# Key-value products of one batch: one wait for two units, or a wait for each

## The chip, the cores and the metric

The kernel runs on one core of a Trainium2 chip. The metric is device time in microseconds (us).

Names in the profile: PE is TensorE, PEld its weight loads, ACT is ScalarE, DVE VectorE, POOL GpSimd, SP SyncE, which issues loads and stores. A name like L540 is line 540 of the kernel. At L540 are the key-value products that this document is about; L705 and L751 are the products with the first and the second weight (line numbers shift by a few from run to run: in the changed kernel these are L541, L703 and L749). `VR` and `VB` are V before and after its cast to bf16, `PS` is a PSUM buffer, `MBLK` the normalized key-value products, `XT` the attention's result, `ESB` the exponentials of the ELU, `qsT` the softmax of Q, transposed. An eviction is a copy out of PSUM.

## The reference, cut to what matters

Linear attention over 8 batches of 8 heads, then two matrix products with an ELU between them:

```python
q_s = softmax(q, axis=-1); k_s = softmax(k, axis=2)         # 576 positions, 64 wide
kv  = np.einsum('bhsd,bhse->bhde', k_s, v)                  # the key-value products
x   = np.einsum('bhsd,bhde->bhse', q_s, kv)                 # then laid out as 4608 x 512
h   = x @ w_in                                              # 512 x 2048
g   = np.where(h > 0, h, np.exp(np.minimum(h, 0)) - 1)
out = g @ w_out                                             # 2048 x 512
```

The last two products are nearly all of the work. The attention of a later batch is worked in between them.

## The kernel before: the parts that matter

A batch is handled as two units of four heads. `kv` records the products of both units as **one** operation of 72 small matmuls (a "stay"), which waits for all that either unit needs:

```python
def kv(self, units, ps, key):
    ...
    def mm(e):
        for x, n in enumerate(units):
            ek, VB = self.ek(n % 2), self.VB[n % 2]
            for c in range(CH):                      # 9 chunks
                for f in range(2):
                    for h in range(2):
                        ...
                        last = e.matmul(P[hs, o:o + D + 1], ek[fs, h, c, :],
                                        VB[fs, h, c, 0:D + 1], start=(c == 0), stop=(c == CH - 1))
        return last
    R = []
    for n in units:
        i = n % 2
        R += [f"kR{i}", f"VB{i}0", f"VB{i}1", f"VBone{i}"]
    S.add("pe", len(units) * 270 + 200, mm, key, R=R, X=self.banks(ps), tag=f"kv{units}")
    # ... DVE takes the reciprocals and forms MBLK from the result
```

`kR` is a unit's exponentials of K (made on ACT), `VB` its V in bf16 (cast on DVE or POOL). A scheduler in Python orders all recorded operations. Its `emit` turns dependencies into semaphores: an operation increments its engine's semaphore only if another one needs to know of it, and the increment rides on the operation's last instruction. I call that increment a mark:

```python
            for d in want:
                if kn.get(d.sem.name, 0) >= d.val:
                    continue                              # already known
                self.E[o.eng].wait_ge(d.sem, d.val)
                ...
            ins = o.emit(self.E[o.eng])
            ...
            elif o in needed:
                count[o.eng] += 1
                o.sem, o.val = sems[o.eng], count[o.eng]
                ins.then_inc(o.sem, 1)
```

After a stay the loads of the next batch's K and V go into the same buffers, so each of them waits for the operation that read the buffer last:

```python
for n in units:
    if more:
        loads(n + 2, "kv", key)       # W=[kR.., vR..]: overwrites what the products read
        self.k_part(n + 2, k1)
```

The softmax here doesn't subtract the row's maximum and nothing guards it: scores larger than these inputs give would overflow.

## Time and profile before

| | before |
|---|---|
| device time, median of 3 | 297.22 us (297.14 to 298.07) |
| span of the profiled execution | 295.2 us |
| PE busy | 289.4 us |
| stays of L540, each of 72 matmuls | 7 |
| wait of PE in them | 0.3 us, in the first stay only |

PE is at work for all but 5.8 us of the span, of which 3.0 us come after its last matmul (it ends at 292.17) and 2.5 us in the first 7.6 us. The question is how much of one short wait can be taken away. A matmul is drawn longer than its share of the time, so sums here are made from starts.

### The profile page before, as it was taken

The numbers are of one execution on the slowest core, as the hardware profiler recorded it, in microseconds if no ns is written. First come the engines' busy times: TensorE is split into PE (matmuls) and PEld (weight loads), VectorE is DVE, ScalarE is ACT, GpSimd is POOL, SyncE is SP. The second block draws the span as 40 slices with busy tenths as digits, with TensorE's granted clock in tenths as the row PEclk, the third lists the DMA queues.
The fourth block names the chain that finished last, engine by engine and source line by source line (L and its number), as shares of the span: only waits on it lengthen the run. The fifth ranks groups of instructions, "written<-read, shape, count | busy, mean of one in ns | idle before, by whom it ended". The sixth has DMA issues, their size and how long they took to land.

```text
span 295.2 us, 4381 instructions
## 1 busy us (share of the span) xinstructions
PE 289.4 (98%) x1836; PEld 235.7 (80%) x1836; DVE 151.1 (51%) x173; ACT 152.9 (52%) x179; POOL 123.0 (42%) x135
## 2 busy tenths in 40 slices
PE   6999999999999999999999999999999999999995
PEld 2688878888888788878888888788878888888885
DVE  6757835898356904782368416760661056105600
ACT  5676447935776175636554655536531454125411
POOL 8996201763177025713472237314740055005500
PEclk9999999999999999999999999999999999999999
DMA  7999979979992696049902990098002110230022
GB/s 254 314 393 389 386 251 308 295 235 160 356 196 76 228 340 136 0 132 350 223 0 58 365 276 6 5 344 197 0 0 67 44 34 2 48 75 21 0 67 76
DMA packets 37747, 49.50 MB, mean 168 GB/s; under 512 B 17312, under 2 KB 18624, under 8 KB 37728
## 3 DMA queue, kind: packets, MB, share of 16 engines
q1 hardware_dynamic: 30992, 34.68, 42.3%
q0 software_dynamic: 6272, 14.03, 15.6%
q10 hardware_dynamic: 464, 0.53, 0.5%
q8 instruction: 14, 0.23, 0.3%
q14 instruction: 5, 0.04, 0.0%
HBM read 36.70 MB, written 9.44 MB: 156 GB/s over the span
## 4 chain that ended last, share of the span: by engine, by line
PE 85%; DMA 7%; POOL 6%; issue 0%; DVE 0%; ACT 0%; POOLq 0%
PE PS L751 41%; PE PS L705 39%; DMA VR<-in_v_dram 7%; POOL W L367 3%; PE PS L540 2%; PE PS L635 2%; PE PS L669 1%; POOL W L378 1%; POOL VR L323 1%; POOL KR L323 0%; POOL QR L355 0%; POOL QR L824 0%; POOL KR L344 0%; DVE VB L489 0%; ACT OSB L784 0%
## 5 line engine op out<-in xcount | busy, mean ns | idle before, releaser
L734 DVE SCALAR_TENSOR_TENSOR GT<-ESB,PS 128x1024 fp32r<-128x1024 f32 x68 | 82.7, 1220 | 111.4 <-POOL ESB L731 111.3
L751 PE MATMUL PS<-W,GT 128*128 128x512 f32 (+1 forms) x592 | 136.5, 386 | 0.0
L705 PE MATMUL PS<-XT,W 128*128 128x512 f32 x576 | 132.8, 390 | 0.0
L705 PEld LDWEIGHTS PS<-XT,W 128*128 128x128 f32 x576 | 107.9, 188 | 22.7 <-issue 0.3
L751 PEld LDWEIGHTS PS<-W,GT 128*128 128x128 f32 x592 | 108.0, 188 | 21.6
L731 POOL TENSOR_SCALAR ESB<-ESB 128x1024 f32<-128x1024 f32 x68 | 71.0, 1047 | 100.4 <-ACT ESB L719 100.3
L719 ACT ACTIVATE ESB<-PS 128x1024 f32<-128x1024 f32 x72 | 73.7, 1028 | 49.2 <-PE PS L705 49.2
L765 ACT ACTIVATE OSB<-PS 128x512 f32<-128x512 f32 x35 | 20.6, 599 | 50.5 <-PE PS L751 50.0
L485 POOL CAST VB<-VR 128x1152 bf16<-128x1152 f32 x12 | 14.6, 1216 | 45.7 <-DMA VR<-in_v_dram 45.7
L418 DVE TENSOR_REDUCE ZQ<-QR 128x18 f32<-128x1152 f32 (+1 forms) x16 | 19.1, 1198 | 3.0 <-ACT QR L412 3.0
L432 DVE TENSOR_TENSOR QS<-QR,RZQ 128x1152 f16<-128x1152 f32 x14 | 18.9, 1360 | 0.3
L479 ACT ACTIVATE KR<-KR 128x1152 bf16<-128x1152 f32 x14 | 15.9, 1169 | 4.3 <-DMA KR<-in_k_dram 4.3
L472 POOL CAST qsT<-QR 128x1152 fp32r<-128x1152 f16 x12 | 13.8, 1148 | 9.0 <-DMA QR<-QS 9.0
L412 ACT ACTIVATE QR<-QR 128x1152 f32<-128x1152 f32 (+1 forms) x16 | 16.2, 1038 | 1.0 <-DMA QR<-in_q_dram 0.9
L655 ACT ACTIVATE XT<-PS 128x640 fp32r<-128x640 f32 (+1 forms) x12 | 8.2, 738 | 15.4 <-PE PS L635 15.4
L367 POOL DMA_DIRECT2D W<-in_moe_w_in_dram x16 | 10.0, 1406 | 0.0
L679 ACT ACTIVATE XT<-PS 128x1024 fp32r<-128x1024 f32 (+3 forms) x8 | 6.8, 847 | 5.7 <-PE PS L669 5.7
L691 PE MATMUL PS<-IDLE 128*128 128x512 f32 (+1 forms) x14 | 7.8, 665 | 1.5 <-DVE IDLE L803 1.5
L378 POOL DMA_DIRECT2D W<-in_moe_w_out_dram x6 | 9.0, 2398 | 0.0
L635 PE MATMUL PS<-qsT,MBLK 128*128 128x320 f32 (+3 forms) x32 | 7.1, 337 | 0.0
L691 PEld LDWEIGHTS PS<-IDLE 128*128 128x128 f32 (+1 forms) x14 | 2.6, 209 | 5.5 <-issue 2.4
L540 PEld LDWEIGHTS PS<-VB,KR 64*64 64x64 bf16 x504 | 4.7, 107 | 2.6 <-DVE GT L734 1.8
(52 smaller groups left out, 95.7 us busy)
## 6 DMA issues: line engine op xcount, KB each, us to landing
out_dram<-OSB SPq DMA_DIRECT2D x67, 128.0 KB, 2.4
QR<-in_q_dram SPq DMA_DIRECT2D x12, 576.0 KB, 7.6
KR<-in_k_dram SPq DMA_DIRECT2D x12, 576.0 KB, 6.2
VR<-in_v_dram SPq DMA_DIRECT2D x12, 576.0 KB, 6.9
W<-in_moe_w_in_dram POOLq DMA_DIRECT2D x16, 256.0 KB, 9.2
W<-in_moe_w_out_dram POOLq DMA_DIRECT2D x3, 1024.0 KB, 15.0
KR<-in_k_dram POOLq DMA_DIRECT2D x3, 576.0 KB, 18.2
VR<-in_v_dram POOLq DMA_DIRECT2D x4, 288.0 KB, 13.4
```

The lines of the kernel that those rows point to most:

```text
L367: "gp", 530, lambda e, kc=kc: e.dma_start(self.W1[:, kc, sl], w[kc, :, :, sl]), key,
L412: lambda e, part=part: e.activation(part, part, AF.Exp), key,
L418: S.add("dve", 1350 if n > 1 else 750, lambda e, z=z, src=src: e.tensor_reduce(z, src, AX.X, ALU.add), key, R=self.q_res(n) if n > 1 else ...
L432: S.add("dve", 1400, lambda e: e.tensor_tensor(qso, raw[:, :, :, :], rz, ALU.mult), key, R=qR + [f"RZQ{i}"], W=[f"QS{al}"], low=True, tag= ...
L479: S.add("act", t_act(1152, False), lambda e: e.activation(ek[:, :, :, :], flat.rearrange("p (h c d) -> p h c d", h=2, c=CH), AF.Exp), key, ...
L485: self.cv[n] = S.add("gp", 1250, lambda e: e.tensor_copy(VB[:, :, :, 0:D], raw[:, :, :, :]), key, R=rv, W=[f"VB{i}0", f"VB{i}1"], low=True ...
L705: last = e.matmul(P[:, t * 512:(t + 1) * 512], self.W1[:, kc, tt * 128:(tt + 1) * 128], self.XT[:, kc, rc:rc + BLK], start=(kc == 0), stop ...
L719: S.add("act", t_act(1024, True), lambda e: e.activation(esb[:, :], P[:, :], AF.Exp), key, W=[f"E{i}"], X=self.banks(ps), tag=f"exp{j}.{g}")
L731: S.add("gp", 1120, lambda e: e.tensor_scalar(esb[:, :], esb[:, :], 1.0, 0.0, ALU.min, ALU.max), key, X=[f"E{i}"], tag=f"min{j}.{g}", port ...
L734: S.add("dve", t_dve(1024), lambda e: e.scalar_tensor_tensor(gt, esb[:, :], -1.0, P[:, :], ALU.add, ALU.max), key, R=[f"E{i}"], W=gw, X=se ...
L751: last = e.matmul(dst, GT[:, jj, ts * 128:(ts + 1) * 128], self.W2[:, jj, cols], start=(jj == 0), stop=(jj == 15))
L765: S.add("act", t_act(512, True), lambda e: e.activation(osb[:, :], src, AF.Copy), key, W=[f"O{i}0", f"O{i}1"], X=[f"b{bk}"], tag=f"evo{jb} ...
```

## The change

Intent: the first unit's 36 products should not stand behind the second unit's V, which arrives later. Each unit's products become an operation of their own. The order of matmuls stays as it was.

```diff
-        def mm(e):
-            for x, n in enumerate(units):
-                ek, VB = self.ek(n % 2), self.VB[n % 2]
+        for x, n in enumerate(units):
+            i = n % 2
+
+            def mm(e, x=x, ek=self.ek(i), VB=self.VB[i]):
                 for c in range(CH):
 ...
-            return last
-        R = []
-        for n in units:
-            i = n % 2
-            R += [f"kR{i}", f"VB{i}0", f"VB{i}1", f"VBone{i}"]
-        S.add("pe", len(units) * 270 + 200, mm, key, R=R, X=self.banks(ps), tag=f"kv{units}")
+                return last
+            S.add("pe", 270 if x else 470, mm, key, R=[f"kR{i}", f"VB{i}0", f"VB{i}1", f"VBone{i}"],
+                  X=self.banks(ps), tag=f"kv{n}")
```

## The prediction

> **What bounds the kernel now.** I began with the page's busy times and its slices, then the chain that ended last in order of time, then the waits of PE alone, then the timeline around the one wait that the change can touch. From the page:
>
> ```profile
> PE 289.4 (98%) x1836; PEld 235.7 (80%) x1836; DVE 151.1 (51%) x173; ACT 152.9 (52%) x179; POOL 123.0 (42%) x135
> ...
> PEclk9999999999999999999999999999999999999999
> ...
> PE 85%; DMA 7%; POOL 6%; issue 0%; DVE 0%; ACT 0%; POOLq 0%
> ```
>
> PE is busy for 289.4 of 295.2 us at an undiminished clock; every other engine stands at about half. The chain is PE for 85%; its 7% of DMA lies wholly before 41 us. This is that joint of the chain (start, length, what):
>
> ```profile
> 20.92 19.92 DMA VR<-in_v_dram
> 40.84 0.02 issue
> 40.86 0.48 DVE VB L489
> 41.34 0.04 issue
> 41.38 0.78 PE PS L540 x68
> 42.16 2.05 PE PS L751 x8
> ```
>
> From 41.38 on the chain never leaves PE until the last eviction at 292.21. Behind the joint PE has nothing to wait for, so whatever PE gains here should come off the end undiminished, and nothing gained elsewhere would. The waits of PE, whole run (total, times, longest):
>
> ```profile
> PE PS L691 <- DVE IDLE L803: 1.5, 1, 1.5
> PE PS L513 <- DVE QS L432: 1.0, 1, 1.0
> PE PS L540 <- DVE VB L489: 0.3, 1, 0.3
> ```
>
> Three waits in 295 us, and only the last belongs to the key-value products (L540). There are seven stays of these products, 72 matmuls each, and six of them show no wait of PE. So one stay of seven can gain, the first one. Its timeline, 36 to 43 us:
>
> ```profile
> 36.35 1.17 ACT L479 ACTIVATE KR<-KR 128x1152 bf16<-128x1152 f32 x1 [3.26 <-DMA KR<-in_k_dram]
> 37.43 0.90 ACT L521 ACTIVATE qsT<-PS 128x896 fp32r<-128x896 f16 x1
> 37.86 0.76 DVE L494 CAST VB<-VR 128x1152 bf16<-128x1152 f32 x1 [0.77 <-DMA VR<-in_v_dram]
> ...
> 39.00 2.08 PE L751 MATMUL PS<-W,GT 128*128 128x512 f32 x8
> 39.37 1.16 ACT L479 ACTIVATE KR<-KR 128x1152 bf16<-128x1152 f32 x1 [1.04 <-DMA KR<-in_k_dram]
> ...
> 40.86 0.47 DVE L489 CAST VB<-VR 128x576 bf16<-128x576 f32 x1 [0.28 <-DMA VR<-in_v_dram]
> ...
> 41.38 0.78 PE L540 MATMUL PS<-VB,KR 64*64 64x65 bf16 x72 [0.30 <-DVE VB L489]
> ...
> 42.09 2.12 PE L751 MATMUL PS<-W,GT 128*128 128x512 f32 x8
> ```
>
> The first unit has its exponentials at 37.52 (36.35 + 1.17) and its V at 38.62 (37.86 + 0.76). The second has its exponentials at 40.53 and the last half of its V at 41.33 (40.86 + 0.47). All 72 matmuls wait for that 41.33.
>
> **What the Trainium skill says.** "TensorE: Matmul & The Clock Gate", section "Step-by-step: what each phase is for": matmuls stay in program order, only weight loads are pulled ahead. The trace agrees: the first unit's 36 products, whose V was ready at 38.62, stood until 41.38 behind a wait placed on the first of the 72. "Perfetto Trace Analysis", section "Tensor Engine Instruction (MATMUL, LD_WEIGHTS)": the end of a matmul in a profile is estimated from its size. It shows here: a 128x512 matmul is drawn 0.389 us long, but 64 of them take 14.51 us in the chain, 0.227 each. So I count from start to start, not by the drawn idle of 0.30. Same page, section "Identifying Dependency Chains": a second awaited engine can cost an inserted EventSemaphore instruction. The trace has such records on PE's sequencer of 0.051 us each (one at 40.57, before this stay), beside running matmuls.
>
> **The change part by part.**
>
> Removed: the first unit's products no longer wait for the second unit's V. When would they start? In the stay at 96.5 us, which has no wait of PE, the matmuls before it end in drawing at 96.60 and L540 starts at 96.53, 0.07 us before. In the first stay the matmuls before end at 41.08 (39.00 + 2.08), so an unhindered start is 41.01. What the first unit needs is there: V at 38.62, exponentials at 37.52, and the PSUM pair, whose last reader before this is the transpose's eviction on ACT, over at 38.33 (37.43 + 0.90).
>
> Moved: 36 of 72 matmuls. From the start of L540 to the start of the next L751 is 42.09 - 41.38 = 0.71 us for 72, so 36 take 0.355. They would run from 41.01 to 41.37. The second unit is let go where all 72 were before, at 41.38, almost exactly when PE is done with the first. It ends its issue at 41.38 + 0.355 = 41.74 in place of 42.09. **Gain: 0.355 us**, which is both the whole of the first unit's products and nearly the whole of the wait (41.38 - 41.01 = 0.37).
>
> Added: one wait of the second unit, on ACT and on DVE. The listing of the changed program shows it in this first stay alone; the other six keep their waits. It may cost one sequencer record of 0.05 us in the middle of the stay. If none of that is hidden, 0.30 is left. One more increment of PE's semaphore per stay; I set it at nothing, since PE's matmuls carry such increments all over the trace without a change of pitch.
>
> Moved by the scheduler: the instruction order on PE, DVE, ACT and SP is unchanged. On POOL three later blocks have the casts of qsT (L472, 1.15 us) one place nearer the front among the clamps of ESB (L731, 1.04 us): clamp, cast, clamp, clamp, cast in place of clamp, clamp, cast, clamp, clamp, cast, and in the last of them both casts ahead of the first clamp. On SP, the reload of each first unit's K waits for the first unit's products alone, so it may go out some 0.36 us earlier, and the second unit's reload has its own wait. Those loads have 20 us before their use.
>
> Sum: -0.355, less at most 0.05: between 0.30 and 0.36 us out of 297.22, **0.1%**.
>
> **The rivals.**
>
> *A transfer takes the place of the wait.* The matmuls after this stay read the last three pieces of the second weight, which queue behind that V. Issue plus time to landing gives 41.52, 42.17 and 43.44 us. PE reaches the first at 42.09 now, and at about 41.74 after the change; the margin shrinks from 0.57 to 0.22. The second is first read four matmuls later (43.12, then 42.77), the third at 44.86 (then 44.5). All three still land first, so I expect no new wait. Against me: a landing 0.3 us later in another run would take 0.1 of the gain. The gain cannot turn into a loss through this: PE would only wait where the same data held it at the latest before.
>
> *POOL becomes the bound through the new cast order.* A cast that waits for its transpose holds back the clamp behind it, and with that the evictions by DVE and PE's PSUM. For it: the transpose before the 112 us block lands at 112.47, and the first clamp of that block starts at 112.50. Against it: the block at 174.76 in the kernel before already has exactly the new order (clamp, cast, clamp, clamp, cast) and PE shows no wait there; between its later clamps POOL idles 0.77 us each, so a shift of half a microsecond is regained within two clamps. In the block with both casts in front, the second transpose landed at 204.66 and the first clamp ran at 205.83, so the second cast would be over at about 205.85. Price if I am wrong: a few tenths of a microsecond each, perhaps 1 us over three blocks.
>
> *The gain is absorbed further on.* What follows on PE needs MBLK (DVE done at 43.32, needed at 43.82) and XT (DVE done at 45.81, weight load at 46.49). Both hang on PE's own progress and move forward with it. What hangs on transfers is done long before: the cast of V for the next stay is over by 60.17 and used at 67.16. I see nothing that gives it back.
>
> *The large win.* The DMA piece of 19.92 us in the chain tempts one to think that a wait of many microseconds is at stake. PE was busy during nearly all of it; the idle end of it is 0.37.
>
> **Range and chances.** 297.22 - 0.33 = **296.9 us**. The three times before spread from 297.14 to 298.07, more than the whole effect, so the range is set by the spread: 296.3 to 297.7. Faster by 2% would need 5.9 us, and all idle of PE in the span is 5.8, most of it in the first slice: chance 0.005. Slower by 2% would need a repeated stall in POOL's blocks of about 1 us in each of six: 0.005. Within 2%: 0.99.
>
> **What would show it.** Right: the first stay splits in two, the first half starting near 41.0 and the second near 41.4, the next L751 at about 41.75; PE's wait for VB gone or under 0.1; all later PE marks 0.3 to 0.36 earlier, the last eviction near 291.9. W2's landings unchanged and no wait of L751 for them. The later stays unchanged in length. Wrong: a wait of L751 for W near 41.8, a wait of PE behind POOL's reordered casts at 112 to 119, 143 to 150 or 205 to 208 us, or a first half that starts no sooner, because a PSUM bank or the sequencer held it.

## The result, and the profile after

| | before | after |
|---|---|---|
| device time, median of 4 | 297.49 us (297.14 to 298.07) | 297.13 us (296.93 to 297.71) |
| ratio, 95% interval | | 0.9989 (0.9966 to 1.0013) |
| span of the profiled execution | 295.2 us | 295.2 us |
| first stay, from the matmul before it to the matmul after it | 1.397 us | 1.097 us |
| stays 2 to 6, from their first matmul to the matmul after them | 0.708 us each | 0.734 us each |
| stay 7, the same | 0.708 us | 0.708 us |

A ratio is the mean time of one kernel's fast runs over that of the other's fast runs of the same rounds, so not quite the ratio of the medians. The interval spans zero difference: **device time does not show whether the change gained anything**. What happened is in the trace. The waits of PE in the changed kernel, whole run (total, times, longest), have lost their third line:

```profile
PE PS L689 <- DVE IDLE L801: 1.5, 1, 1.5
PE PS L513 <- DVE QS L432: 1.0, 1, 1.0
```

The first stay in the timeline of the changed kernel (start, length, engine, line; L541 are the products, L749 the second weight):

```profile
41.00 0.47 DVE L489 CAST VB<-VR 128x576 bf16<-128x576 f32 x1 [0.28 <-DMA VR<-in_v_dram]
41.16 0.85 PE L541 MATMUL PS<-VB,KR 64*64 64x65 bf16 x72
41.94 0.97 PE L749 MATMUL PS<-W,GT 128*128 128x512 f32 x3
```

The products now start while the cast of V still runs (it ends at 41.468). Before, they started 0.05 us after it. The chain by engine has lost its DMA of 7%:

```profile
PE 96%; DMA 1%; DVE 1%; ACT 0%; SPq 0%; issue 0%
```

So far all is as intended: 0.300 us gained in the stay. But the chain of the changed kernel, in order of time, also shows the later stays (here the third and the last):

```profile
96.45 0.73 PE PS L541 x71
97.18 6.62 PE PS L749 x28
...
220.99 0.71 PE PS L541 x71
221.70 6.61 PE PS L749 x28
```

and the same place in the kernel before:

```profile
96.60 0.71 PE PS L540 x71
97.31 6.61 PE PS L751 x28
```

The third stay costs 0.73 where it cost 0.71, and the last one does not. (A record or two of a stay's 72 are missing from some chain pieces; the starts of single matmuls give 0.734 and 0.708.) It is the same in stays 2 to 6: 5 x 0.026 = 0.13 us given back.

From the matmul ahead of the first stay to the issue of the last store, right behind the last eviction, the changed kernel takes 251.768 us, the kernel before 251.928: **0.160 us less**. That is 0.300 gained, 0.131 lost in five stays, and 0.009 lost in the rest. It is one execution of each kernel, and the rest varies too: in e5b below, whose stays 2 to 7 have no mark in the middle either, the stretch from stay 2 on took 0.167 us less than in the kernel before. The lengths of the stays, on which the argument rests, repeat within 0.003 in all runs. In absolute times not even the 0.160 shows: the last eviction of the chain starts at 292.19 against 292.21, because PE came to the first stay 0.145 us later in this execution (40.840 against 40.695). That began with the load of q's second half, which landed at 4.60 us against 4.34.

### The profile page after: what moved, and what is told of

It is laid out like the page before. It is cut to its first block, busy times and chain, and to the rows that moved or that the text cites. A ratio compares the mean times of both kernels' runs of the same rounds, so it can differ in the third digit from the quotient of the medians.

```text
span 295.2 us, 4383 instructions
## 1 busy us (share of the span) xinstructions
PE 289.7 (98%) x1836; PEld 236.0 (80%) x1836; DVE 150.8 (51%) x173; ACT 153.0 (52%) x179; POOL 123.6 (42%) x135
## 4 chain that ended last, share of the span: by engine, by line
PE 96%; DMA 1%; DVE 1%; ACT 0%; SPq 0%; issue 0%
PE PS L749 45%; PE PS L703 44%; PE PS L633 2%; PE PS L541 2%; PE PS L667 1%; DMA QR<-in_q_dram 1%; PE PS L689 1%; PE PS L513 1%; PE PS L599 0%; DVE QS L432 0%; DVE ZQ L418 0%; ACT QR L412 0%; SPq L822 0%; ACT OSB L782 0%; PE PS L581 0%
## 5 line engine op out<-in xcount | busy, mean ns | idle before, releaser
L749 PE MATMUL PS<-W,GT 128*128 128x512 f32 (+1 forms) x592 | 136.5, 386 | 0.0
L749 PEld LDWEIGHTS PS<-W,GT 128*128 128x128 f32 x592 | 108.0, 188 | 21.6
L485 POOL CAST VB<-VR 128x1152 bf16<-128x1152 f32 x12 | 15.3, 1278 | 43.7 <-DMA VR<-in_v_dram 43.7
L541 PEld LDWEIGHTS PS<-VB,KR 64*64 64x64 bf16 x504 | 4.9, 107 | 2.2 <-DVE GT L732 1.8
```

The source lines that it names most:

```text
L485: self.cv[n] = S.add("gp", 1250, lambda e: e.tensor_copy(VB[:, :, :, 0:D], raw[:, :, :, :]), key, R=rv, W=[f"VB{i}0", f"VB{i}1"], low=True ...
L749: last = e.matmul(dst, GT[:, jj, ts * 128:(ts + 1) * 128], self.W2[:, jj, cols], start=(jj == 0), stop=(jj == 15))
```

## The experiments

Three things were open. What lengthens stays 2 to 6: the mark in mid-stay, the reloads of K that go out earlier, or the moved casts on POOL? Why did the first stay gain 0.300 and not 0.355? And is that gain bounded by the wait, by the first unit's own time, or by something else? All twelve runs gave correct results. Nine of them (all but e1, after_again and e9) were executed once, for their trace alone, so their state is on record as unknown; their device times are not used, and their granted clocks lie between 0.994 and 1.000. Diffs below are against the changed kernel, unless said otherwise.

The table reads the first stay of each run in the same way, without the first run of e6a, whose V was cast long before PE came. "Cast" is how long after the matmul ahead of the stay the last cast of V ended; this differs between executions, since PE and the loads run against each other. "Stay" runs from that matmul to the matmul that follows the products.

| run | wait | cast | stay | stay less cast | 36th to 37th matmul |
|---|---|---|---|---|---|
| before | for both | 0.635 | 1.397 | 0.762 | 0.021 |
| after | split | 0.628 | 1.097 | 0.469 | 0.073 |
| after_again | split | 0.666 | 1.135 | 0.469 | 0.111 |
| e1_one_mark | split | 0.449 | 1.087 | 0.638 | 0.062 |
| e3_marks_alone | for both | 0.637 | 1.425 | 0.788 | 0.021 |
| e4_six_marks | split | 0.276 | 1.104 | 0.828 | 0.062 |
| e5b_spin_before | for both | 0.635 | 1.399 | 0.764 | 0.021 |
| e5a_spin_after | split | 0.678 | 1.320 | 0.642 | 0.062 |
| e6b_late_v_before | for both | 0.943 | 1.706 | 0.763 | 0.021 |
| e6a_again | split | 0.853 | 1.321 | 0.468 | 0.298 |
| e9_one_sem | split | 0.633 | 1.104 | 0.471 | 0.078 |
| e10_two_waits | for both | 0.676 | 1.497 | 0.821 | 0.060 |
| e11_one_wait | for both | 0.692 | 1.455 | 0.763 | 0.023 |

### The changed kernel again, and without the mark

e1_one_mark lets the reloads wait for the second unit's products, so nobody needs to know of the first unit's, and `emit` puts no mark on them:

```diff
-            S.add("pe", 270 if x else 470, mm, key, ...
+            op = S.add("pe", 270 if x else 470, mm, key, ...
+            if x == 0:
+                head = op
+        for res in S.parts([f"kR{units[0] % 2}"]) + [f"VB{units[0] % 2}{h}" for h in range(2)]:
+            S.r[res] = [op if d is head else d for d in S.r[res]]
```

> The changed kernel with one thing undone: the reloads of the first unit's K and V wait for the second unit's products again, so PE's semaphore is no longer incremented in the middle of a stay; the split wait of the first stay is kept. The order of instructions on all engines is that of the kernel before. Theory of the mark (an increment on a matmul in mid-stay costs PE 0.026 us): the stays at 67, 96, 127, 158 and 190 us take 0.708 from their start to the next matmul as before, not 0.734, and the last eviction comes 0.30 us nearer to the first stay than in the kernel before, not 0.16. The first stay still gains 0.29 to 0.32. Rival (the six later stays are longer because of where they now stand against the transfers, whatever the marks): they stay at 0.734. Device time: 0.1% under the kernel before at most, inside the spread.

> The changed kernel unaltered, beside the others on this chip. Both theories: the first stay from the matmul before it to the matmul after it takes 1.10 us (1.40 before), the five stays after it 0.734 (0.708 before), the last one 0.708; net 0.14 to 0.18 us nearer the end, in device time under the spread of a few tenths of a us.

Measured: in after_again stays 2 to 6 took 0.734 or 0.735 again and the last 0.708. From the matmul ahead of the first stay to the issue of the last store it took 251.762 us, 0.166 less than the kernel before, as expected, but by another sum: its first stay took 1.135 and not the 1.10 expected, since V's cast ended later against PE (0.666), and 0.045 was gained in a stretch between the first two stays that the change does not touch. In e1_one_mark all six later stays took 0.708 or 0.709, and that stretch 251.576; its first stay took 1.087. Its timeline at the third stay:

```profile
96.36 0.78 PE L541 MATMUL PS<-VB,KR 64*64 64x65 bf16 x72
97.07 1.21 PE L753 MATMUL PS<-W,GT 128*128 128x512 f32 x4
```

Device time, 5 rounds: e1_one_mark 296.86 us median against 297.38 (ratio 0.9989, 0.9976 to 1.0002); after_again 297.04 (ratio 0.9997, 0.9979 to 1.0015). Neither is clear of zero. What follows: taking the mark away takes the 0.026 away. But e1 also sends the reload out later and has POOL's old order, so this alone does not name the mark. Nor are 251.576 against 251.928 a clean comparison: in e1 V was cast early (0.449), so its first stay had little to wait for, and 0.04 of the difference lies in stretches that the change does not touch and that vary between executions.

### Marks alone, and more marks

e3_marks_alone keeps everything of the kernel before, the order on every engine included, and only records a stay as two operations that both wait for both units and both carry a mark:

```diff
-            S.add("pe", ..., R=[f"kR{i}", f"VB{i}0", f"VB{i}1", f"VBone{i}"],
+            S.add("pe", ..., R=[f"{t}" for u in units for t in (
+                f"kR{u % 2}", f"VB{u % 2}0", f"VB{u % 2}1", f"VBone{u % 2}")],
...
+        needed |= {o for o in seq if o.eng == "pe" and o.tag.startswith("kv")}
```

> The kernel before with marks alone: the stay is recorded as two operations, both waiting for both units, and both increment PE's semaphore; the wait is not split and no reload goes out earlier; the order on all engines is that of the kernel before. Theory of the mark: the first stay starts 0.69 us after the matmul before it, as before, and takes about 0.734; all the six others, the last included, take 0.734 in place of 0.708, so the end comes about 0.18 us later against the first stay. Rival (earlier reloads of K, or the new order of casts on POOL, lengthen the stays): 0.708 everywhere.

e4_six_marks is the changed kernel with `for c0 in (0, 3, 6)` around the recorded operation, so six operations of 12 matmuls to a stay, each with its mark.

> The changed kernel with each stay recorded as six operations of 12 matmuls, each with its increment: five marks in mid-stay in place of one, in the same order of matmuls, with the wait split as in the changed kernel. Theory of the mark, each one at a full 0.026: the later stays take 0.708 + 5 x 0.026 = 0.84 us. The same theory with 0.009 in mid-stay for each and 0.017 once at the end: about 0.77. Rival (reloads or POOL's order, unchanged against the changed kernel): 0.734, and 0.708 in the last stay.

Measured: e3 took 0.734 or 0.735 in all seven stays, the first and the last included, and its stretch was 252.136 us, 0.208 longer than before (0.18 expected; 0.183 lies in the stays). Its wait for V stood as before:

```profile
PE PS L542 <- DVE VB L490: 0.3, 1, 0.3
```

Its last stay shows the cost, 0.73 in place of 0.71:

```profile
221.17 0.80 PE L542 MATMUL PS<-VB,KR 64*64 64x65 bf16 x72
221.90 0.74 PE L751 MATMUL PS<-W,GT 128*128 128x512 f32 x2
```

e4 took 0.786 in each of the six later stays, 0.078 over 0.708. Its last stay:

```profile
221.48 0.86 PE L543 MATMUL PS<-VB,KR 64*64 64x65 bf16 x72
222.27 0.50 PE L752 MATMUL PS<-W,GT 128*128 128x512 f32 x1
222.45 0.18 DVE L551 RECIPROCAL RZK<-PS 128x4 f32<-128x4 f32 x1 [1.08 <-PE PS L543]
```

What follows: **the mark is the cause**. In e3 no reload went out earlier and POOL's order was the old one, and the 0.026 came all the same, even in the last stay, where the changed kernel needs no mark and pays nothing. The rivals fall. The starts show where the 0.026 goes: 0.009 more from the first to the last matmul, and 0.017 more from the last one to the matmul after the stay. With five marks these were 0.061 and 0.017. So PE's starts do not pay the full 0.026 for each mark; e4's outcome lies near the second of the two sizes I had written down (0.77), a little above.

The cost does not fall where the mark stands. In the third stay of the changed kernel all starts up to the 67th matmul, the 37th included, lie within 0.001 of those of the kernel before, and in e4 those up to the 43rd, though three marks stand before it. The other engines see the full sum: in the third stay PE's semaphore update at the end comes 0.820 us after the first product in the kernel before, 0.846 in e3 and 0.950 in e4, so 0.026 later for one more mark and 0.130 for five, 0.026 each. In the last stay, where DVE is free, its reciprocal shows it: it starts 0.84, 0.87 and 0.97 after the first product (222.45 - 221.48 in e4). Why PE's next starts pay less than this, and why they pay so late, stays open.

Where PE pauses in mid-stay anyway, as in every split first stay, the mark cost nothing that can be seen: with V cast early the 72 products took 0.769 to the next matmul without a mark (e1) and 0.766 with it (the first run of e6a), and PE's update at the end came after 0.869 in both.

### A needless wait in mid-stay

In e1 the cast of V was over 0.22 us before the 37th matmul, and still 0.062 us passed from the 36th matmul to the 37th, against 0.021 in an unsplit stay. The second unit waits for two engines, ACT and DVE, and the trace shows an inserted EventSemaphore record of 0.051 us there. e10_two_waits and e11_one_wait put two or one needless waits, long satisfied, in the middle of every stay of the kernel before:

```diff
+            if o.again:     # the second unit's operation; no mark on the first
+                ...         # held: the units' exponentials (ACT) and V casts (DVE or POOL)
+                for d in ...:                          # both, or ACT's alone
+                    self.E[o.eng].wait_ge(d.sem, d.val)
```

> The kernel before, its wait unsplit and no marks, with two needless waits in the middle of every stay, on ACT and on another engine, for values that the start of the stay has already waited for. Theory (an inserted wait record costs PE 0.04 and the restart 0.02): the gap between the 36th and 37th matmul is 0.06 in every stay, and every stay takes 0.77 in place of 0.708. Rival (a satisfied wait costs nothing, the 0.06 was waiting for V): 0.02 and 0.708.

> The same with one needless wait, on ACT alone, which rides on the matmul's own weight load. Theory of the record: 0.02 to 0.03 and 0.71 to 0.73 in every stay. Rival (any wait breaks the stream): 0.06 and 0.77.

Measured: e10 0.060 to 0.062 from the 36th to the 37th matmul, and 0.766 to 0.769 for each of the seven stays; e11 0.021 to 0.023, and 0.708 or 0.709. The third stay of e10, then of e11:

```profile
96.85 0.84 PE L547 MATMUL PS<-VB,KR 64*64 64x65 bf16 x72
97.62 0.73 PE L761 MATMUL PS<-W,GT 128*128 128x512 f32 x2
```

```profile
96.86 0.78 PE L547 MATMUL PS<-VB,KR 64*64 64x65 bf16 x72
97.57 0.74 PE L761 MATMUL PS<-W,GT 128*128 128x512 f32 x2
```

From 96.85 to 97.62 is 0.77, from 96.86 to 97.57 is 0.71. What follows: one satisfied wait, on ACT, is free (0.001 at most); a second one, on another engine, brings the inserted record and costs 0.060 us in this stream of small matmuls: 0.040 as a gap, and 0.021 because after such a pause 36 matmuls take 0.291 where they take 0.270 in the unbroken stream. No run puts a satisfied wait on that other engine alone, so the record is told from the engine by the trace only: e10 has one such record in each stay, e11 has none. So with a wait for two engines the split of the first stay costs 0.06, even when nothing is left to wait for.

### One engine to wait for in place of two

e9_one_sem is e1 with the last half of V cast only after ACT's exponentials of that unit (`after=[ex] if h else ()`), so that the word of DVE covers both.

> The version with one mark, and in it the last half of the second unit's V is cast after that unit's exponentials, so that PE waits in mid-stay for one engine, with no inserted wait record. The gap between the 36th and 37th matmul is 0.06 with the record even when nothing is left to wait for. Theory (the record costs PE 0.04): where V's cast ends less than 0.57 us after the matmul before the stay, the gap falls to 0.02 to 0.03 and the stay takes 0.71 to 0.73 us; where it ends later (0.63), the cast decides, the 37th matmul comes 0.05 after it, and nothing is gained over the version with one mark. Rival (any wait in mid-stay costs the same): gap 0.06 and stay 0.77 in both cases.

Measured: V was cast late in the profiled execution (0.633), the 37th matmul came 0.054 after the cast, and the stay took 1.104 us. That is the second of the two expected cases: nothing gained over e1 where the cast decides. The first case did not come up in it, so the benefit of the single wait is shown by e11 and not by e9. The later stays took 0.707 to 0.710. Device time: 296.95 us against 297.24, ratio 0.9992 (0.9978 to 1.0006), so the same. If one is to be kept, it is e1 or e9: in the trace they keep the gain of the first stay and pay nothing later. Device time proves neither faster than either kernel.

### Using up the wait, and stretching it

e5 puts one idle matmul ahead of the first stay, in the kernel before (e5b) and in the changed one (e5a). Its length in the scheduler's model is set to nothing, so that no order changes:

```diff
+                    if units[0] == 2:
+                        self.spin(1, 2 * ps)
```

> The kernel before with one idle matmul (128x512 fp16 into the stay's own PSUM bank, overwritten afterwards) put in front of the first stay, some 0.22 us of PE's time. Theory (the stay is bound by the cast of the second unit's V): hidden in the wait; from the end of that cast to the first matmul of the stay 0.05 us, and the stay itself 0.71, as before. Rival (PE needs that time for a drain or a switch of its own before the stay): everything 0.22 later.

> The changed kernel with the same idle matmul in front of the first stay. Theory (gain is the wait, but at most the first unit's own issue time of about 0.31 us): 0.22 us of the wait of 0.37 is now used up, so against the kernel before with the idle matmul the stay gains only about 0.13 (0.15 less one mark), and the second unit no longer waits: the gap between the 36th and 37th matmul falls from 0.073 to 0.02 to 0.03. Rival (a fixed gain from starting earlier): 0.30 as without it.

The first stay of e5b, then of e5a:

```profile
41.30 0.39 PE L691 MATMUL PS<-IDLE 128*128 128x512 f16 x1
41.76 0.78 PE L540 MATMUL PS<-VB,KR 64*64 64x65 bf16 x72
42.47 0.50 PE L751 MATMUL PS<-W,GT 128*128 128x512 f32 x1
```

```profile
41.04 0.39 PE L689 MATMUL PS<-IDLE 128*128 128x512 f16 x1
41.36 0.84 PE L541 MATMUL PS<-VB,KR 64*64 64x65 bf16 x72
42.13 0.73 PE L749 MATMUL PS<-W,GT 128*128 128x512 f32 x2
```

Measured: in the kernel before, the idle matmul cost nothing (1.399 against 1.397, counted from the last matmul of the second weight). With the change it left 1.320, a gain of 0.079. I had expected 0.13, and the gap in mid-stay to fall to 0.02 or 0.03; it fell to 0.062 only. The missing part is the 0.060 of the inserted record: 0.371 of wait, less 0.230 used up, less 0.06, is 0.08. The two executions are not at an equal place of the cast (0.635 and 0.678). e5a's stay does not hang on it, V having been cast 0.225 before the 37th matmul, so 0.079 is the gain at e5b's place; at e5a's own an unsplit stay would take 0.678 + 0.764 = 1.442, and the gain would be 0.122. The gap in mid-stay is the same in both readings. The rival of a fixed gain falls.

e6 makes V late: `"dve" if n == 3 else vconv` in place of `"halves"`, so V is cast in one piece of 0.765 us after both halves have landed.

> The kernel before with the second unit's V cast as one piece after both halves have landed, 0.76 us in place of 0.47 after the last half. Theory: the stay starts 0.05 after that cast, 0.29 to 0.30 us later than in the kernel before, about 0.98 us after the matmul before it; from there on everything is 0.3 later against it.

> The changed kernel with the same later V: the wait of the unsplit stay would be about 0.66 us. Theory (gain capped by the first unit's own issue time, less the restart): the stay gains 0.29 to 0.31 against the kernel before with the later V, no more than with the earlier V, and the gap between the 36th and 37th matmul grows from 0.073 to about 0.37. Rival (the gain is the whole wait): about 0.6.

> The changed kernel with the later V once more: in its first run the first load of q landed 2 us late (6.45 us), PE came to the stay after V was cast, and nothing could be read. As before: with the cast of V ending some 0.9 us after the matmul before the stay, theory (gain capped by the first unit's own issue time of 0.31 us, less the mid-stay cost): the stay gains 0.29 to 0.30 against the kernel before with the later V (1.706 us there, so about 1.41), and the gap between the 36th and 37th matmul is about 0.37. Rival (the gain is the whole wait): 1.09.

Measured: e6b took 1.706, 0.309 longer than before. The first run of e6a told nothing of this: q's second half landed at 6.45 us, PE came to the stay at 43.80, when V had been cast at 41.991, and the run took 299.76 us. Its repetition took 1.321, with the cast ending 0.09 earlier against PE than in e6b (0.853, 0.943); so the gap of about 0.37 that I expected came out as 0.298. At an equal place of the cast that is 0.295 gained, as with the earlier V; the rival of 0.6 falls. Its first stay:

```profile
40.81 0.77 DVE L494 CAST VB<-VR 128x1152 bf16<-128x1152 f32 x1 [2.25 <-DMA VR<-in_v_dram]
41.04 1.07 PE L541 MATMUL PS<-VB,KR 64*64 64x65 bf16 x72
42.04 0.74 PE L749 MATMUL PS<-W,GT 128*128 128x512 f32 x2
```

The products begin before the cast is a third done and pause within it: the 72 matmuls are drawn as one piece of 1.07 us in place of 0.78, and the pause of 0.298 before the 37th lies in that.

The table's column "stay less cast" sums this up. Where the cast decides, the unsplit stay ends 0.762 to 0.764 after it (0.054 to wake, 0.708 for the stay), the split one 0.468 to 0.471 after it (0.054 to wake, 0.291 for 36 matmuls, 0.124 to the next matmul). **The gain is 0.293** (0.291 to 0.296 over these runs), whatever the wait's length, as long as the second unit's cast is what it waits for.

## Why the prediction was right or wrong, point by point

- *Which stay can gain.* Right: only the first did, and PE's wait for VB is gone.
- *Unhindered start at 41.01, that is 0.32 us after the matmul ahead (40.695).* Right: 0.318, the distance that most later stays have too.
- *36 matmuls take half of 0.71, so 0.355.* The wrong term. Of the 0.708 of a stay, 0.125 lies between the last product and the next matmul and is paid once, however the stay is cut. The first unit's part is 0.313 (0.291 and a gap of 0.021), and the second, restarted, takes 0.021 longer than in the stream. So 0.293 in place of 0.355.
- *A record of 0.05 in mid-stay, at most.* The size was fair: 0.060 in e10. In the changed kernel most of it ran beside the wait for V: the 37th matmul came 0.054 after the cast there and in e9, which has no record, alike. The 0.300 of the stay is the 0.293 and 0.007 of an earlier cast. My lower bound of 0.30 was met, by the wrong term and the luck of 0.007.
- *One more increment per stay: nothing.* Wrong, and the larger miss. I argued from marks on 128x512 matmuls, where no change of pitch is to be seen (0.226 or 0.227 us from start to start at L705 from 47 to 61 us, with a mark on every eighth). In a stream of small ones a mark cost 0.026 per stay; five stays gave back 0.131 of 0.300. So "the later stays unchanged in length" was wrong too.
- *The transfer as the new wait.* It did not come: that piece of the second weight landed at 41.66 in the changed kernel and PE reached it at 41.94.
- *K's reload some 0.36 us earlier.* In the third stay it went out 0.54 us after the first product in place of 0.84, so 0.30 earlier. By itself it hurt nothing in the stays, which take 0.734 with it and, in e3, without it; but the mark is its price.
- *POOL's new order.* Harmless, as argued: no wait of PE behind POOL in the changed kernel, and e1 and e3, with the old order, do not differ in the stays but by the mark.
- *Idle of PE: 5.8 us, most of it in the first slice.* Wrong, without consequence: 3.0 of it come after the last matmul, where no wait can be taken away.
- *Absorbed further on.* I saw nothing that would give the gain back; something did, on PE itself.
- *The end.* All of PE was to come 0.30 to 0.36 us earlier from the first stay on; 0.160 is what the trace shows at the end. The time of 296.9 with its range holds the 297.13, but the spread of the runs, not the sum, is what put it there. The start of a run alone (the landing of q between 4.3 and 6.5 us) moves it more than the change does.

## What to carry to other kernels

Before splitting an operation to start half of it early, count what the cut itself costs on the bound engine in every place where the code runs, not only where the wait is: here one stay gained 0.300 us and five others, which had no wait to lose, paid 0.026 each. Cut where there is a wait, leave later consumers on the last part's word so that the first part needs no mark, and let a wait in the middle of small matmuls be for one engine. Half of an operation is not half of its time when a fixed tail is paid once.

## What the Trainium skill lacked or had wrong

- "TensorE: Matmul & The Clock Gate", section "The cost: per-tile semaphore tail", puts each increment after packed matmuls at 26.3 ns. The runs agree, counted to PE's semaphore update at the end of the third stay: 0.026 us later for one more increment (e3), 0.130 for five (e4). What the section lacks is the delay of the matmul that follows: 0.026 for one, 0.078 and not 0.130 for five.
- "Perfetto Trace Analysis", section "Identifying Dependency Chains", tells of inserted EventSemaphore instructions but not of their cost. In a stream of 64x65 matmuls one such record, its waits long satisfied, cost 0.060 us (e10), a single wait without a record nothing (e11).
- No page that I read has the time of a stream's restart: 36 of these matmuls took 0.291 us after a pause and 0.270 when they ran on.
